# Attention's uses of one PSUM bank set apart, two activations kept on chip, and splits and conversions spread

## The chip, the cores and the metric

One core of a Trainium2 chip. The metric is the device time of one execution in microseconds (us). TensorE is called PE, VectorE DVE, ScalarE ACT, GpSimd POOL and SyncE SP in the rows.

## What is computed

Sliding-window attention for 4 batches of 8 heads (576 positions, 64 per head), then two feed-forward networks over the 2304 tokens:

```python
scores = scale * np.matmul(q, k.transpose(0, 1, 3, 2))
# heads 0-3: 0 <= rel < 32; heads 4-7: 0 <= rel < 128 and rel % 4 == 0
attn = softmax(np.where(masks, scores, -1e9))
x = (attn @ v).transpose(0, 2, 1, 3).reshape(2304, 512)
h = x @ w_in1                                     # 512 -> 2048
x = (np.maximum(h, 0) + alpha * np.minimum(h, 0)) @ w_out1
h = x @ w_in2
g = np.where(h >= 1, h, np.where(h <= -1, 0, (h + 1) ** 2 / 4))
out = g @ w_out2
```

All is float32.

## The kernel before

**Splits.** Every matrix factor is cut into a high and a low part (`two`: ACT copies the high part at L329, DVE or POOL subtracts it at L330), and each product is three matmuls: L514 to L516 for a plain hidden product H, L545 to L547 for a hidden product of the 7-product scheme, L679 to L681 for an output product Y. `xv` is split x, `wr` and `woh`/`wol` are split weights, `gh`/`gl` a split activation.

**Tiles.** The tokens are cut into tiles (network, number): (0,0) 512, (0,1) 256, (0,2) 512, (0,3) 1024, (1,0) 1024, (1,1) 1024, (1,2) 256 tokens. There are 16 feature blocks f per tile.

**Slots.** Tiles (0,0), (0,1), (0,2) run in 16 slots each. A slot f is: H of block f (`f_h`), an attention point, the activation of f (`f_g`: ACT L644, DVE L647, ACT L654; `f_cut` L660 subtracts), Y of block f-2 (`f_y`), another attention point. The 18 attention groups after batch 0 are spread over these points by two tables: `STARTS` says at which point a group's scores begin, `STAGES` how many points later its further steps come. A group is: `s_ps` (scores, PE L147; DVE adds the mask at L151, takes the maximum at L154, subtracts it at L160, ACT takes exp at L161), `t_ps` (PE L214 turns the probabilities, ACT L216 copies them to `pT`), `o_ps` (PE L225 by v; DVE L231 to L233 normalises), `x_ps` (PE L240 turns back; ACT L258 copies to `XA`). All four PE results of every group use one and the same PSUM bank, tag "a".

**Weights.** Network weights arrive on SP's in-order queue (`st`, L274), DVE rewrites the bits of each with three integer operations (`w_cut`, `conv`: L323, L324, L317), and results that are needed later go to DRAM (`whole<-wf`, L301) and come back (`wb<-whole` L351, `wo<-whole` L1075).

**Pairs.** (0,3), (1,0) and (1,1) are computed as two halves of 512 tokens with seven products in place of eight. `x_seven` makes and splits the sums of x (DVE L453 makes a sum in `room`, `two` splits it); `more_x(k)` issues k pieces of that list. Eight steps `p_h` make two feature blocks each for both halves; the first half's Y are issued between, the second half's activations go to DRAM (`gd<-XA`, L624) and are read back (`gx<-gd`, L629) for a "second half" of 16 Y blocks. The first half's last Y and the second half's first ones stand at the border between. In the first pair's second half DVE also converts the last weights of the second network; `HELD` lists the blocks that are not converted there.

**Last.** (1,2) runs in slots again.

Each engine runs its instructions in the order in which the program issues them.

Of the kernel before, what the change touches and what calls it, by code (L numbers as in the profile page):

```python
# [22 lines left out]
P = 128  # L23
# [41 lines left out]
STARTS = (1, 6, 10, 14, 18, 22, 26, 30, 37, 43, 49, 55, 61, 66, 70, 74, 78, 82)  # L65
STAGES = ((3, 4, 6), (2, 3, 5), (3, 5, 8))
# [4 lines left out]
HELD = [f for f in range(NF) if f < 4 or f >= NF - 2]  # L71
# [15 lines left out]
def attention_then_two_ffns(ctx: ExitStack, tc: tile.TileContext, a0, aqk, av, w1i, w1o, w2i, w2o, alpha, masks, ident, out):  # L87
# [68 lines left out]

    def a_exp(i):
        src, s, mx = sc_t.pop(i)
        if i < 4 * NGB:
            nc.vector.tensor_tensor(s, src, mx[:, :, None].to_broadcast([P, 2 * GS, KEYS]), ALU.subtract)  # L160
            nc.scalar.activation(s, s, AF.Exp, scale=SCALE)  # L161
            s_t[i] = s
            return
        nc.vector.tensor_scalar(mx, mx, -SCALE, None, ALU.mult)
        for n in range(2 * GS):
            nc.scalar.activation(s[:, n], src[:, n], AF.Exp, bias=mx[:, n:n + 1], scale=SCALE)
        s_t[i] = s
# [214 lines left out]
    def p_weights(n, p, i):  # L382
# [7 lines left out]
        def other(j):  # L390
            t = wt[n, p, j] = r_slot((n, p, j))
            if n == PAIRS[2]:
                nc.sync.dma_start(t.bitcast(F32), kept[p, j])
                return
            two(t[:, 0], t[:, 1], sums[n, p][:, 2 * j - 2:2 * j].rearrange("p a b -> p (a b)"), on)
            if n == PAIRS[1]:
                kept[p, j] = kept_p.tile([P, 2, DM], F32, tag=f"k{p}_{j}", name="kept")
                nc.sync.dma_start(kept[p, j], t.bitcast(F32))
# [34 lines left out]
    def x_seven(n, room):  # L433
# [13 lines left out]
        def plain(i, k, j, m):  # L447
            return lambda: split(i, m, src(k, j, m), nc.vector if n == PAIRS[0] and i > 3 else nc.gpsimd)
# [80 lines left out]
    def p_h(q, p, after, between):  # L529
# [32 lines left out]
        def top(j, k):  # L562
# [39 lines left out]
        product(c, 2, 1, 5, False)  # L602
        act(1, 0, d)
# [5 lines left out]
        between(2)  # L609
        top(0, 1)  # L610
# [14 lines left out]

    def g_load(n, f):
        tag = x_free.pop(0)
        t = pools[tag].tile([P, 2, TW], F32R, tag=tag, name="gx")
        nc.sync.dma_start(t.bitcast(F32), gd[n, f])  # L629
        gt[(n, 1), f] = (t[:, 0], t[:, 1])  # L630
        g_tags[n, f] = tag
# [30 lines left out]
    def f_y(key, f):  # L662
# [7 lines left out]
        if f == 0:  # L670
# [5 lines left out]
        for c in range(NC):  # L676
            o = yt[key][c][:, :w]
            cs = slice(c * P, (c + 1) * P)
            nc.tensor.matmul(o, wl[:, cs], gh[:, :w], start=(f == 0), stop=False)  # L679
            nc.tensor.matmul(o, wh[:, cs], gh[:, :w], start=False, stop=False)  # L680
            nc.tensor.matmul(o, wh[:, cs], gl[:, :w], start=False, stop=(f == NF - 1))  # L681
        if part:
            x_free.append(g_tags.pop((n, f)))
        if f == NF - 1:
# [18 lines left out]
    with tc.manual_schedule(), ExitStack() as late:  # L703
# [66 lines left out]
        def start(i):  # L770
            a_scores(i, ps_a, "a", i < 2 * NGB)
            a_load_qk(i + 2)
            a_exp(i)
# [113 lines left out]
        def slot(n, f, k):  # L887
# [66 lines left out]
        for n in PLAIN:  # L954
            for f in range(NF):
                slot(n, f, k)
                k += 1
                if n == PLAIN[0] and f == NF - 3:
# [6 lines left out]
                if n == PLAIN[2] and f == READY - 1:  # L965
                    assert nxt == NG and not at
# [4 lines left out]
        def step(q, p):  # L971
            n = PAIRS[q]
            split_pending()
            end = p == NF // 2 - 1

            def after(i):
                if not end:
                    for k in ((0,), (1, 2), (3,))[i]:
                        p_weights(n, p + 1, k)
                if i == 0:  # L980
# [3 lines left out]
                    if end:  # L984
                        for f in range(3):
                            g_load(n, f)
                elif i == 1 and end:
                    one_y()
                    wo_split((n, 0), NF - 2)
                elif i == 2:  # L990
                    if q == 0:
                        more()

            p_h(q, p, after, lambda k: conv(k) if q == 0 else None)

        for q, n in enumerate(PAIRS):
# [16 lines left out]
            flush()  # L1013
            wo_split((n, 0), NF - 1)
            one_y()
            wo_split((n, 1), 0)
            one_y()
            wo_split((n, 1), 1)
            turn = iter(range(1 << 30))

            def room():
                pool, tag = banks(q, 1)[next(turn) % NC]
                return pool.tile([P, TW], F32, tag=tag, name="room")

            if q == 0:
                w0_tile[0] = room
# [3 lines left out]
                more()  # L1030
# [4 lines left out]
            loaded = 3  # L1035
            if nn in PAIRS:
                x_free.extend(r_free[:2])
                del r_free[:2]
            for f in range(NF):
                if loaded < NF:  # L1040
                    g_load(n, loaded)
                    loaded += 1
                if f + 2 < NF:
                    wo_split((n, 1), f + 2)
                if f == NF - 2:
# [3 lines left out]
                    else:  # L1049
                        pend_y += [((n, 1), f), ((n, 1), f + 1)]  # L1050
# [3 lines left out]
                if nn in PAIRS:  # L1054
                    if f in (5, 13):
                        w_base(nn[0], f // 13)
                    if f == NF - 3:
                        r_free.extend(x_free[:2])
                        del x_free[:2]
                    elif f in (8, 9, 10, 11):  # L1060
                        p_weights(nn, 0, f - 8)
                else:
                    if f == 0:
# [109 lines left out]
```

## Time and profile before

| | |
|---|---|
| median of 3 runs | 886.89 us (885.58 to 887.21) |
| the profiled execution | 881.87 us |
| its span | 880.1 us |
| its mean granted clock | 0.994 |
| PE busy | 839.0 us (95%) |
| DVE, ACT, POOL busy | 552.8, 433.6, 487.8 us |

The profiled execution is 5.0 us shorter than the median of the runs. Its span leaves 41.1 us in which PE has no matmul under way. The waits that PE's instructions show say where most of these lie and what ended each.

### The profile page before, as it was taken

To read this page: it belongs to the slowest core of one execution; us is meant where nothing else is said; L and a number is where in the kernel's file an instruction comes from. 1 tells how busy PE (TensorE), PEld (TensorE's weight loads), DVE (VectorE), ACT (ScalarE), POOL (GpSimd) and SP (SyncE) were. 2 spreads that over 40 slices of the span, in tenths; PEclk is the share of its full clock that TensorE was granted. 3 is DMA by queue.
4 is the path that set the end of the run, shared out by engine and by line. 5 is a ranking of instruction groups with operands and counts; after the bars stand their busy time and mean duration, and the time that the engine had idled before them with its cause. 6 is when DMAs were issued, how large, how long until landed. Compare 5 with 4: busy or idle time off the path is not lost.

```text
span 880.1 us, 14306 instructions
## 1 busy us (share of the span) xinstructions
PE 839.0 (95%) x5328; PEld 688.4 (78%) x5330; DVE 552.8 (63%) x911; ACT 433.6 (49%) x809; POOL 487.8 (55%) x417
## 2 busy tenths in 40 slices
PE   6889997998999999999998999999999999999998
PEld 3667776887777778888876788887788888878898
DVE  4788885653776678676558677676417767640143
ACT  3444444555443555555444356554434545453364
POOL 2455554667343656767467677672772242447486
PEclk9999999999999999999999999999999999999999
DMA  7877644553652013543368663625853553549120
GB/s 291 249 223 224 210 137 151 175 182 104 184 174 86 25 42 127 189 145 144 120 251 316 234 228 137 222 96 192 340 186 130 224 186 131 189 163 351 69 90 25
DMA packets 57045, 152.71 MB, mean 174 GB/s; under 512 B 5776, under 2 KB 13584, under 8 KB 56976
## 3 DMA queue, kind: packets, MB, share of 16 engines
q1 hardware_dynamic: 56688, 151.63, 50.6%
q8 instruction: 42, 0.69, 0.3%
q14 instruction: 27, 0.22, 0.1%
q10 hardware_dynamic: 288, 0.16, 0.1%
HBM read 104.59 MB, written 47.19 MB: 172 GB/s over the span
## 4 chain that ended last, share of the span: by engine, by line
PE 83%; DVE 7%; ACT 4%; issue 2%; POOL 1%; DMA 1%; ACTq 0%; DVEq 0%
PE y L679 13%; PE y L681 13%; PE y L680 13%; PE h_ps L545 8%; PE h_ps L547 8%; PE h_ps L546 8%; PE h_ps L514 5%; PE h_ps L516 4%; PE h_ps L515 4%; PE o_ps L225 2%; PE s_ps L147 1%; PE t_ps L214 1%; POOL wol L330 1%; ACT woh L329 1%; DMA st<-w2o 1%
## 5 line engine op out<-in xcount | busy, mean ns | idle before, releaser
L330 POOL TENSOR_TENSOR wol<-wo,woh 128x512 fp32r<-128x512 f32 x159 | 207.3, 1312 | 98.3 <-ACT woh L329 97.6
L679 PE MATMUL y<-gh,wol 128*128 128x512 f32 (+1 forms) x444 | 163.7, 369 | 4.8 <-POOL wol L330 4.8
L681 PE MATMUL y<-gl,woh 128*128 128x512 f32 (+1 forms) x444 | 160.3, 361 | 0.0
L680 PE MATMUL y<-gh,woh 128*128 128x512 f32 (+1 forms) x444 | 160.1, 361 | 0.0
L330 POOL TENSOR_TENSOR wr<-wb,wr 128x512 fp32r<-128x512 f32 x60 | 77.7, 1294 | 129.9 <-ACT wr L329 129.8
L545 PE MATMUL h_ps<-xv,wr 128*128 128x512 f32 x336 | 131.1, 390 | 1.1 <-POOL wr L330 0.9
L329 ACT ACTIVATE woh<-wo 128x512 fp32r<-128x512 f32 x159 | 96.8, 627 | 69.1 <-PE y L681 53.3
L547 PE MATMUL h_ps<-xv,wr 128*128 128x512 f32 x336 | 130.8, 389 | 0.0
L546 PE MATMUL h_ps<-xv,wr 128*128 128x512 f32 x336 | 130.8, 389 | 0.0
L330 POOL TENSOR_TENSOR wr<-wi,wr 128x512 fp32r<-128x512 f32 x50 | 64.7, 1295 | 101.4 <-ACT wr L329 101.3
L679 PEld LDWEIGHTS y<-gh,wol 128*128 128x128 f32 x444 | 83.8, 189 | 21.8 <-POOL wol L330 7.4
L681 PEld LDWEIGHTS y<-gl,woh 128*128 128x128 f32 x444 | 83.7, 188 | 13.3
L514 PE MATMUL h_ps<-xv,wr 128*128 128x512 f32 (+1 forms) x256 | 91.8, 359 | 2.1 <-DVE g L647 1.8
L680 PEld LDWEIGHTS y<-gh,woh 128*128 128x128 f32 x444 | 83.8, 189 | 12.2
L515 PE MATMUL h_ps<-xv,wr 128*128 128x512 f32 (+1 forms) x256 | 87.4, 342 | 0.2 <-DVE xv L330 0.2
L516 PE MATMUL h_ps<-xv,wr 128*128 128x512 f32 (+1 forms) x256 | 87.3, 341 | 0.0
L679 PE MATMUL y<-gx,wol 128*128 128x512 f32 x192 | 75.6, 394 | 4.0 <-DMA gx<-gd 3.2
L559 ACT ACTIVATE g<-g,half 128x512 f32<-128x512 f32 x64 | 44.8, 723 | 69.1 <-DVE g L558 67.8
L680 PE MATMUL y<-gx,woh 128*128 128x512 f32 x192 | 75.3, 392 | 0.0
L545 PEld LDWEIGHTS h_ps<-xv,wr 128*128 128x128 f32 x336 | 63.1, 188 | 15.6 <-POOL wr L330 1.3
L681 PE MATMUL y<-gx,woh 128*128 128x512 f32 x192 | 75.3, 392 | 0.0
L547 PEld LDWEIGHTS h_ps<-xv,wr 128*128 128x128 f32 x336 | 63.1, 188 | 13.2
(123 smaller groups left out, 1505.5 us busy)
## 6 DMA issues: line engine op xcount, KB each, us to landing
gd<-XA SPq DMA_DIRECT2D x48, 512.0 KB, 4.4
gx<-gd SPq DMA_DIRECT2D x48, 512.0 KB, 6.0
wb<-whole SPq DMA_DIRECT2D x30, 512.0 KB, 4.8
st<-w1i SPq DMA_DIRECT2D x16, 512.0 KB, 4.2
st<-w1o SPq DMA_DIRECT2D x16, 512.0 KB, 5.0
st<-w2i SPq DMA_DIRECT2D x16, 512.0 KB, 4.9
st<-w2o SPq DMA_DIRECT2D x16, 512.0 KB, 4.4
kept<-wr SPq DMA_DIRECT2D x16, 512.0 KB, 2.7
```

The costliest lines, as they stand in the source:

```text
L329: nc.scalar.activation(hi, src, AF.Copy)
L330: low_on.tensor_tensor(lo, src, hi.bitcast(F32), ALU.subtract)
L514: nc.tensor.matmul(ps[:, :w], r[:, 1, cs], x[:, 0, xs], start=(c == 0), stop=False)
L515: nc.tensor.matmul(ps[:, :w], r[:, 0, cs], x[:, 1, xs], start=False, stop=False)
L516: nc.tensor.matmul(ps[:, :w], r[:, 0, cs], x[:, 0, xs], start=False, stop=(c == NC - 1))
L545: nc.tensor.matmul(o, w[:, 1, cs], x[:, 0], start=start and m == 0, stop=False, skip_group_check=not start)
L546: nc.tensor.matmul(o, w[:, 0, cs], x[:, 1], start=False, stop=False, skip_group_check=not start)
L547: nc.tensor.matmul(o, w[:, 0, cs], x[:, 0], start=False, stop=m == 1, skip_group_check=not start)
L559: nc.scalar.activation(t, t, AF.Square, bias=half, scale=0.5)
L679: nc.tensor.matmul(o, wl[:, cs], gh[:, :w], start=(f == 0), stop=False)
L680: nc.tensor.matmul(o, wh[:, cs], gh[:, :w], start=False, stop=False)
L681: nc.tensor.matmul(o, wh[:, cs], gl[:, :w], start=False, stop=(f == NF - 1))
```

## The change

1. **Attention points.** `STARTS` and `STAGES` are replaced, so that two uses of bank "a" never follow one another without an H or a Y block between them.
2. **exp.** `a_exp` is cut in two: DVE's subtraction stays with the scores (`a_less`), ACT's exp is issued one attention point later, behind the copy of an `x_ps` that may stand there.
3. **Second halves.** They begin with blocks 14 and 15 (`SECOND`), whose activations stay in buffers of split x (`g_home`); these two are neither stored nor loaded, and their `woh`/`wol` are those of the first half. So `gd` and `gx` go from 48 to 42 transfers each, and six weight splits fall away. The split of the next weights, and the last two Y of the first half, come earlier, in the last step.
4. **Conversions.** `HELD` is 8 blocks in place of 6, so 8 conversions are left for the first pair's second half in place of 10; their loads are issued by a schedule of their own into two more buffers.
5. **Store of kept weights.** `kept<-wr` is issued a step later (`later`).
6. **Splits of x.** The four of (0,1) are spread over the last four slots of (0,0); two staging buffers are freed three slots earlier. `plain` of (0,3) goes to POOL throughout, that of (1,0) to DVE for its last two products. In the last slots of (0,2) the weights come ahead of `more_x`.

```diff
-STARTS = (1, 6, 10, 14, 18, 22, 26, 30, 37, 43, 49, 55, 61, 66, 70, 74, 78, 82)
-STAGES = ((3, 4, 6), (2, 3, 5), (3, 5, 8))
+STARTS = (1, 6, 10, 14, 18, 22, 26, 31, 37, 43, 49, 55, 61, 67, 71, 75, 79, 83)
+STAGES = {1: (3, 4, 6), 26: (3, 4, 6), 31: (3, 5, 7), 37: (3, 5, 7), 43: (3, 5, 7), 49: (3, 5, 7), 55: (3, 5, 7), 61: (2, 3, 7)}
...
-HELD = [f for f in range(NF) if f < 4 or f >= NF - 2]
+HELD = [f for f in range(NF) if f < 2 or f >= NF - 6]
+SECOND = [NF - 2, NF - 1] + list(range(NF - 2))
...
     def a_exp(i):
-        src, s, mx = sc_t.pop(i)
-        if i < 4 * NGB:
-            nc.vector.tensor_tensor(s, src, mx[:, :, None].to_broadcast([P, 2 * GS, KEYS]), ALU.subtract)
-            nc.scalar.activation(s, s, AF.Exp, scale=SCALE)
...
+        nc.scalar.activation(s_t[i], s_t[i], AF.Exp, scale=SCALE)
...
-            return lambda: split(i, m, src(k, j, m), nc.vector if n == PAIRS[0] and i > 3 else nc.gpsimd)
+            return lambda: split(i, m, src(k, j, m), nc.vector if n == PAIRS[1] and i > 3 else nc.gpsimd)
...
+            elif p == NF // 2 - 1:
+                t = g_home(n, f)
+                hi, lo = t[:, 0], t[:, 1]
...
-            if k:
+            if k and p < NF // 2 - 1:
                 later.append(lambda: g_keep(n, f, XA[:, 2 * j:2 * j + 2, t0:t0 + TW]))
...
+        i = SECOND.index(f) if part else f
+        if n in PAIRS and not part and f in SECOND[:2]:
+            wos[(n, 1), f] = (wh, wl)
...
-                stages = STAGES[2 if 2 * NF <= at[i] < 4 * NF - 4 else 0 if i in (NGB, 2 * NGB) else 1]
+                stages = STAGES.get(at[i], (2, 3, 5))
+                if k == 1:
+                    a_exp(i)
...
-            if n == PLAIN[0] and f == NF - 1:
-                for c in range(NC):
-                    x_split(nn, c)
-            if n == PLAIN[1] and f >= NF - NC:
-                x_split(nn, f - NF + NC, True)
+            if n in PLAIN[:2] and f >= NF - NC:
+                x_split(nn, f - NF + NC, n == PLAIN[1])
...
+                if NF - 4 <= f < NF - 1:
+                    p_weights(nn, 0, f - NF + 4)
                 if f in (9, 10):
                     more_x(3)
                 elif f >= READY:
-                    more_x(5 if f < NF - 1 else len(x_work))
-                if f >= NF - 4:
-                    p_weights(nn, 0, f - NF + 4)
+                    more_x((5, 5, 6, len(x_work))[f - READY])
+                if f == NF - 1:
+                    p_weights(nn, 0, 3)
...
                 elif i == 1 and end:
                     one_y()
                     wo_split((n, 0), NF - 2)
+                    wo_split((n, 0), NF - 1)
+                elif i == 3 and end:
+                    one_y()
+                elif i == 4 and end:
+                    wo_split((n, 1), 0)
...
-            flush()
-            wo_split((n, 0), NF - 1)
             one_y()
-            wo_split((n, 1), 0)
             one_y()
-            wo_split((n, 1), 1)
...
                 if q == 0:
+                    for _ in range((2, 1, 1, 0, 0, 1, 1, 1, 1)[i] if i < 9 else 0):
+                        w_load(*pend_l.pop(0))
```

What it moves, word for word from the order of instructions. PE at the end of tile (0,1), where a group's `x_ps` and the next group's `t_ps` stand; before:

```order
L681 MATMUL y_2021<-gl,woh 128x256
L240 MATMUL x_ps<-idt,o 128x128 x3
L214 MATMUL t_ps<-idt,s 128x128 x3
L514 MATMUL h_ps<-xv,wr 128x512
L515 MATMUL h_ps<-xv,wr 128x512
L516 MATMUL h_ps<-xv,wr 128x512
```

and in the changed kernel (its lines are L237 for L240, L211 for L214, L513 to L515 for L514 to L516, L688 to L690 for L679 to L681):

```order
L515 MATMUL h_ps<-xv,wr 128x256
L237 MATMUL x_ps<-idt,o 128x128 x3
L688 MATMUL y_2012<-gh,wol 128x256
L689 MATMUL y_2012<-gh,woh 128x256
L690 MATMUL y_2012<-gl,woh 128x256
...
L690 MATMUL y_2015<-gl,woh 128x256
L211 MATMUL t_ps<-idt,s 128x128 x3
L513 MATMUL h_ps<-xv,wr 128x512
```

`t_ps` followed `x_ps` at once; now the Y block of 12 matmuls stands between them.

ACT in a slot of tile (0,2), where exp stood ahead of the slot's activation; before:

```order
L161 ACTIVATE s<-s 128x384
L644 ACTIVATE g<-h_ps 128x512
L654 ACTIVATE gh<-h_ps 128x512
L329 ACTIVATE wr<-wi 128x512
L258 ACTIVATE XA<-x_ps 128x96x4
L329 ACTIVATE woh<-wo 128x512
L216 ACTIVATE pT<-t_ps 128x384
```

and in the changed kernel (L255 is the copy of `x_ps`, L164 exp, L650 and L660 the activation, L326 a split's copy, L213 the copy of `t_ps`):

```order
L255 ACTIVATE XA<-x_ps 128x96x4
L164 ACTIVATE s<-s 128x384
L650 ACTIVATE g<-h_ps 128x512
L660 ACTIVATE gh<-h_ps 128x512
L326 ACTIVATE wr<-wi 128x512
L213 ACTIVATE pT<-t_ps 128x384
L326 ACTIVATE woh<-wo 128x512
```

Both are one group's pass: exp and the copy of the earlier group's `x_ps` have become neighbours ahead of the activation.

SP at the border of the first pair's halves; before:

```order
L301 DMA whole<-wf 128x1024
L624 DMA gd<-XA 256x1x512 x4
L629 DMA gx<-gd 128x1024 x3
L624 DMA gd<-XA 256x1x512 x2
L274 DMA st<-w2o 128x1024 x2
L629 DMA gx<-gd 128x1024
L1075 DMA wo<-whole 128x512
```

and in the changed kernel (L298 stores `wf`, L637 loads `gx`, L271 loads `st`, L1099 reads `wo` back):

```order
L298 DMA whole<-wf 128x1024
L271 DMA st<-w2o 128x1024
L628 DMA gd<-XA 256x1x512 x4
L637 DMA gx<-gd 128x1024 x2
L298 DMA whole<-wf 128x1024
L271 DMA st<-w2o 128x1024 x2
L1099 DMA wo<-whole 128x512
L637 DMA gx<-gd 128x1024
```

The last store of `wf` has come to stand right ahead of the first read-back of `wo`, and two `gx` are issued ahead of it where three were.

## Rows read from the trace of the kernel before

**Rows 1.** The page: busy time, share of the span and instructions of each engine.
```profile
PE 839.0 (95%) x5328; PEld 688.4 (78%) x5330; DVE 552.8 (63%) x911; ACT 433.6 (49%) x809; POOL 487.8 (55%) x417
```

**Rows 2.** Waits of PE, whole span: waiting line <- releaser: us, times, longest.
```profile
PE t_ps L214 <- ACT XA L258: 8.7, 6, 2.7
PE y L679 <- POOL wol L330: 4.8, 4, 1.6
PE s_ps L147 <- issue: 3.3, 1, 3.3
PE y L679 <- DMA gx<-gd: 3.2, 2, 1.7
PE o_ps L225 <- ACT pT L216: 3.1, 2, 2.5
...
PE s_ps L147 <- ACT XA L258: 1.2, 2, 0.9
...
PE y L679 <- POOL wr L330: 0.8, 1, 0.8
```

**Rows 3.** Timeline of DVE at 134 us: start, duration, what, [idle before].
```profile
134.75 3.22 DVE L330 TENSOR_TENSOR xv<-XA,xv 128x256 fp32r<-128x256 f32 x4 [1.10 <-ACT xv L329]
```

**Rows 4.** Timeline of ACT and PE at 214 us.
```profile
214.03 0.48 ACT L258 ACTIVATE XA<-x_ps 128x384 f32<-128x384 f32 x1
...
214.56 0.55 PE L214 MATMUL t_ps<-idt,s 128*128 128x128 f32 x3 [2.73 <-ACT XA L258]
```

**Rows 5.** Busy time by stretch: us, PE, PEld, DVE, ACT, POOL, PEclk, DMA, GB/s.
```profile
214.80:219.20 4.40, 4.40 (x15) 3.50 (x14) 0.00 (x0) 1.01 (x2) 2.17 (x2) 0.61 0.02 4
```

**Rows 6.** Timeline of ACT at 41 us, in the first interleaved group.
```profile
40.67 0.53 ACT L161 ACTIVATE s<-s 128x384 f32<-128x384 f32 x1 [0.51 <-DVE s L160]
41.26 0.64 ACT L329 ACTIVATE wr<-wi 128x512 fp32r<-128x512 f32 x1
```

**Rows 7.** Timeline of ACT and PE at 113 us, an undisturbed group.
```profile
113.05 0.53 ACT L258 ACTIVATE XA<-x_ps 128x192 f32<-128x192 f32 x2
...
115.24 0.49 PE L214 MATMUL t_ps<-idt,s 128*128 128x128 f32 x3
```

**Rows 8.** Timeline of PE, DVE, ACT and POOL, 282.8 to 287.4 us, in slots of (0,2).
```profile
282.85 0.48 PE L514 MATMUL h_ps<-xv,wr 128*128 128x512 f32 x1
...
284.17 0.69 DVE L660 TENSOR_TENSOR gl<-h_ps,gh 128x512 fp32r<-128x512 f32 x1
...
284.73 1.29 POOL L330 TENSOR_TENSOR wr<-wi,wr 128x512 fp32r<-128x512 f32 x1 [6.60 <-ACT wr L329]
284.77 1.80 DVE L453 TENSOR_TENSOR room<-XA 128x512 f32<-128x512 f32 x1
...
285.46 0.39 PE L516 MATMUL h_ps<-xv,wr 128*128 128x512 f32 x1
...
286.61 0.60 ACT L329 ACTIVATE xv<-room 128x512 fp32r<-128x512 f32 x1 [1.43 <-DVE room L453]
287.10 0.55 ACT L258 ACTIVATE XA<-x_ps 128x192 f32<-128x192 f32 x2
287.24 0.69 DVE L330 TENSOR_TENSOR xv<-room,xv 128x512 fp32r<-128x512 f32 x1 [0.66 <-ACT xv L329]
```

**Rows 9.** Timeline of POOL and PE at 315 us, the last slots of (0,2).
```profile
314.93 1.74 POOL L330 TENSOR_TENSOR wol<-wo,woh 128x512 fp32r<-128x512 f32 x1
...
316.72 0.50 PE L679 MATMUL y<-gh,wol 128*128 128x512 f32 x1
```

**Rows 10.** Waits of SP's queue, 440 to 492 us, the first pair's second half.
```profile
SPq L274 <- DVE wo L317: 17.6, 7, 4.3
```

**Rows 11.** Waits of SP's queue, whole span.
```profile
SPq L351 <- DMA whole<-wf: 4.1, 2, 2.1
```

**Rows 12.** Tile `gx`, 466 to 492 us: its seven transfers.
```profile
DMA to landing us min/median/max: 5.2/6.4/7.5
```

**Rows 13.** Timeline of DVE at 449 us, a sum made in the second half.
```profile
449.32 0.69 DVE L453 TENSOR_TENSOR room<-XA 128x512 f32<-128x512 f32 x1
```

More of the change, by code (lines that the diff above doesn't have):

```diff
@@ L155, in a_scores, with a_less @@
         sc_t[i] = (src, s, mx)
+    def a_less(i):
+        src, s, mx = sc_t.pop(i)
+        nc.vector.tensor_tensor(s, src, mx[:, :, None].to_broadcast([P, 2 * GS, KEYS]), ALU.subtract)
+        s_t[i] = s
     def a_exp(i):
-        src, s, mx = sc_t.pop(i)
-        if i < 4 * NGB:
-            nc.vector.tensor_tensor(s, src, mx[:, :, None].to_broadcast([P, 2 * GS, KEYS]), ALU.subtract)
-            nc.scalar.activation(s, s, AF.Exp, scale=SCALE)
[L162 to L167, printed above, removed]
+        nc.scalar.activation(s_t[i], s_t[i], AF.Exp, scale=SCALE)
     def e_scores(i):
@@ L396, in other, with keep @@
             if n == PAIRS[1]:
-                kept[p, j] = kept_p.tile([P, 2, DM], F32, tag=f"k{p}_{j}", name="kept")
-                nc.sync.dma_start(kept[p, j], t.bitcast(F32))
+                def keep():
+                    kept[p, j] = kept_p.tile([P, 2, DM], F32, tag=f"k{p}_{j}", name="kept")
+                    nc.sync.dma_start(kept[p, j], t.bitcast(F32))
+                later.append(keep)
         if i == 0:
@@ L602, in p_h @@
         product(c, 2, 1, 5, False)
+        after(3)
         act(1, 0, d)
@@ L609, in p_h @@
         between(2)
+        after(4)
         top(0, 1)
@@ L957, in attention_then_two_ffns @@
                 k += 1
[L958 removed]
+                if n == PLAIN[0] and f == NF - 6:
                     spare += [0, 0]
@@ L965, in attention_then_two_ffns @@
                 if n == PLAIN[2] and f == READY - 1:
-                    assert nxt == NG and not at
+                    assert nxt == NG and not s_t and not pT_t
                     assert not pend_w and not todo and not cv, (pend_w, todo)
@@ L974, in step @@
             end = p == NF // 2 - 1
+            if end and n != PAIRS[2]:
+                x_free.extend(r_free[:2])
+                del r_free[:2]
             def after(i):
                 if not end:
-                    for k in ((0,), (1, 2), (3,))[i]:
+                    for k in ((0,), (1, 2), (3,), (), ())[i]:
                         p_weights(n, p + 1, k)
@@ L984, in after @@
                     if end:
-                        for f in range(3):
-                            g_load(n, f)
+                        g_load(n, 0)
                 elif i == 1 and end:
@@ L989, in after @@
                     wo_split((n, 0), NF - 2)
+                    wo_split((n, 0), NF - 1)
[3 more added lines that the diff above has]
+                    wo_split((n, 1), 0)
                 elif i == 2:
+                    if end:
+                        g_load(n, 1)
                     if q == 0:
+                        if end:
+                            conv(3)
                         more()
-            p_h(q, p, after, lambda k: conv(k) if q == 0 else None)
+            p_h(q, p, after, lambda k: conv(k) if q == 0 and not end else None)
         for q, n in enumerate(PAIRS):
@@ L1029, in attention_then_two_ffns @@
                 pend_w += rest
-                more()
+                for _ in range(2):
+                    st_free.append(x_free.pop())
+                hold = True
             if nn in PAIRS:
@@ L1034, in attention_then_two_ffns @@
                 x_work += [(lambda c=c: x_split(nn, c, True)) for c in range(NC)]
[L1035 to L1041, printed above, removed]
+            loaded = 4
+            for i, f in enumerate(SECOND):
+                if i and loaded < NF:
+                    g_load(n, SECOND[loaded])
                     loaded += 1
-                if f + 2 < NF:
-                    wo_split((n, 1), f + 2)
-                if f == NF - 2:
+                if 1 <= i < NF - 2:
+                    wo_split((n, 1), SECOND[i + 2])
+                if i == NF - 2:
                     more_x(len(x_work))
@@ L1075, in attention_then_two_ffns @@
                         nc.sync.dma_start(wo[1, f], whole[1, 1, f // 2][:, f % 2])
-                    if f + 1 not in HELD:
+                    if i < NF - 1 and SECOND[i + 1] not in HELD:
                         conv(3)
-                    if f == NF - 4:
+                    if i == NF - 4:
                         assert not pend_w and not todo and not cv
```

56 lines of the change are left out of this document (31 added, 25 removed).

## The prediction

> **What bounds the kernel now.** The page comes first: PE is busy for 839.0 us of the span, no other engine for more than 553 [rows 1]. So the time is PE's work plus PE's gaps, and an edit off PE pays only where PE waits for it. The gaps are read next, from the waits of PE over the whole span [rows 2]. There the reader is to see four families. One is attention's bank: `t_ps` waits 8.7 us in six places and `s_ps` 1.2 us in two for ACT's copy of the `x_ps` that used the bank just before, and one `s_ps` waits 3.3 us. The second is the splits at the border of the halves: Y waits for `wol` on POOL, 4.8 us in four. The third is the read-back: Y waits for `gx`, 3.2 us in two, and once 0.8 us for POOL's `wr` right behind. The fourth is `o_ps`, 3.1 us in two, for ACT's `pT`.
>
> Then the timeline shows what each was waiting behind. The 3.3 us wait has no releaser named ("issue"), but while it lasts DVE makes four low parts of x in a row, 3.22 us, ahead of the normalisation that frees the bank [rows 3]. The longest `t_ps`, 2.73 us, starts right after ACT's copy of `x_ps` at 214.03, and that copy stood behind the slot's own activation and a split [rows 4]. After this wait PE's granted clock was 0.61, a mean of its two levels, 1.2 and 2.4 GHz, for a stretch of 4.40 us [rows 5]; a block of 12 matmuls takes 2.8 us at the full one (first to last start 2.61 us, and one more step of 0.23) [rows 8]. That is about 1.7 us more than the wait itself.
>
> **The change part by part.**
>
> *Bank uses apart.* Nothing is added on PE; the same matmuls stand in another order. Where `t_ps` or `s_ps` followed `x_ps` at once, a block of 2.8 us (1.4 for 256 columns) now lies between, and on ACT the copy stands ahead of the slot's activation, behind which it ran up to 2.7 us late. So I take off the whole of 8.7 + 1.2 us [rows 2] and the 1.7 us of slow clock. The 3.3 us go too: a Y block stands there now, and the four splits of x are one in a slot. Of `o_ps`, 2.5 us is the first group's, whose order doesn't change, and 0.6 goes. Sum: 8.7 + 1.2 + 3.3 + 0.6 + 1.7 = 15.5 us. The bounds are nothing and these 15.5.
>
> *exp later on ACT.* The instructions are the same, in another place. In an undisturbed group ACT's copy of `x_ps` starts at 113.05 and takes 0.53, and `t_ps` starts at 115.24 [rows 7]. exp, 0.53 long [rows 6], behind that copy would be over near 114.2, some 1.0 us ahead. The slot's activation starts 0.5 us later for it, and its Y is two slots off, so nothing waits. The first group is the exception: exp ran at 40.67 and a split's copy (0.64) right behind it [rows 6]. Now the copy, which waits for its converted weight, stands ahead, and exp ends some 0.5 us later than `t_ps` can bear. I add 0.5 us (bounds nothing and 1.2, the copy and exp together).
>
> *New neighbours.* At the start of tile (0,1) `pT` stands behind two copies of splits, 0.6 each: I add 0.8 us (bounds nothing and 1.3). In slots 9 to 11 of (0,2) scores now start after slot 9's Y. DVE's mask add then stands behind that slot's low part, the sum and its split: from 284.17 to 287.93 these took 3.76 us [rows 8]. With the mask add of some 0.55 the bank is free 4.3 us after the low part starts. On PE the scores (about 0.8) and one H, 2.8, lie between. If the low part starts 0.7 us behind `s_ps`, one conversion, `x_ps` waits 4.3 + 0.7 - 3.6 = 1.4 us. I add this; the bounds are nothing and 2.1, for two conversions. One slot on `pT` stands behind the copy of a sum, where `XA` stood before (286.61, then 287.10, [rows 8]); that mirrors the `t_ps` wait of 1.9 us in this place, with exp ahead too but the copy begun earlier. I add 1.2 (bounds nothing and 1.9).
>
> *Weights ahead of x in the last slots of (0,2), and four splits more on POOL.* Before, `wol` ended at 316.67 and its Y started at 316.72 [rows 9], with no time to spare. Two splits of x are now ahead of it on POOL in that slot, 1.29 each (as the split at 284.73, [rows 8]), of which POOL's idle time takes part. I add 1.0 us (bounds nothing and 2.6).
>
> *The border of the halves.* `wol` for blocks 14 and 15 is made two steps of the program earlier, and there is none to be made for the second half's first two Y, which reuse them. So the 4.8 us go [rows 2], 0.7 of it by the same spread in (0,1). The two `gx` waits of 3.2 us came while SP stood for 17.6 us at `st`, whose buffers come free with DVE's conversions, with `gx` queued behind it [rows 10]. Two more buffers, two conversions less and an issue schedule of its own take them away, and with them the wait for `wr` behind, 0.8. Sum 8.8 us, bounds 4.8 (the reads stay late) and 8.8. The six pairs of transfers saved save nothing by themselves: no wait is for a busy queue. What is moved past others on SP is the last store of `wf`, and a read-back of it follows at once. SP stands there until the store has landed; two such waits took 4.1 us [rows 11]. The third `gx` is queued behind. It needs 2.1 + 6.4 us, 7.5 at the slowest [rows 12], and about 1 us of issues: 9.5 to 10.6. Four Y blocks, 14, 15, 0 and 1, cover it with 11.2 us. So it costs nothing, but has under 2 us to spare.
>
> *The rest.* The kept store issued later, on SP, lies beside a step of p_h and delays no load that PE waits for now: nothing. The branch with six small exps ran for no group.
>
> *Sum.* 15.5 + 8.8 = 24.3 us off; 0.5 + 0.8 + 1.4 + 1.2 + 1.0 = 4.9 us on; net 19.4 us less. The profiled execution, 881.87 us, becomes 862.5. The median of the runs shown is 5.0 us above it, and I carry the difference over: 886.89 - 19.4 = 867.5 us.
>
> **A rule against the change.** A sum of x took 1.80 us on DVE while POOL was at a split that had started at 284.73 [rows 8], and 0.69 with POOL idle [rows 13]. So putting four splits on POOL while DVE makes sums can cost 1.1 us each time they meet, 4.4 us of DVE's time, and 867.5 + 4.4 = 871.9 us if PE waited for all of it. I don't take it into the sum, since the sums in slot 9 and 10 are priced at 1.80 already and the later ones have POOL's chain, not DVE's, as the last. The Trainium skill (SBUF — State Buffer, section "Who interferes with whom") has this as a rule: a DVE instruction with two SBUF inputs contends with a GpSimd instruction that reads SBUF, and the later one is blocked until the other is through. The two rows above agree with it: POOL's split ended at 286.02, and the sum 0.55 us after.
>
> **The rivals.**
>
> *Slower: exp in front of the activation.* The place is every one of the 18 groups. ACT must do the copy and exp before the activation, and `t_ps` comes up to two blocks later. Rows 7 leave about 1.0 us. If exp ended 2.6 us later than I say, each `t_ps` would wait 1.6 us: 886.9 - 24.3 + 18 x 1.6 = 891.4 us. It decides from 24.3 / 18 = 1.35 us per group. For it: ACT was late by up to 2.7 us in six groups [rows 2]. Against it: those were late by the slot's own activation, which is now behind exp, not ahead. 7 in 100, and 4 more for half of it, no change.
>
> *The waits move on.* PE's stalls in the slots come back at other points, as they do in slots 10 and 11: half of the 15.5 us is lost, 19.4 - 7.7 = 11.7 net, 875 us. For it: DVE and ACT have no less to do. Against it: PE has slack of a block wherever the order is changed. 13 in 100. If no new wait comes at all, it is 24.3 us less, 862.6: 13 in 100.
>
> *The read-back doesn't get better.* `gx` stays late or SP's wait for `whole` makes the third late: 4.0 us of the gain stay, 871.5 us. For it: under 2 us to spare. 13 in 100. *DVE and POOL meet*, as above, 871.9: 5 in 100.
>
> **How the numbers follow.** The forecast, 865 to 870, has 45 in 100. The range of 8 in 10 leaves out the slower case and no change, and part of the half gain: 859 to 879. A change of 0.2% (1.8 us) is about what can be told. Faster: 45 + 13 + 13 + 13 + 5 = 89, of which I give 1 to the same; same 5; slower 7.
>
> **What would show it.** Right: no `t_ps` or `s_ps` waits for L255 in the slots; no Y waits for `wol` or `gx` at the borders; PE's waits in the slots shrink to `o_ps` and one `x_ps` for DVE near slots 9 to 11 of (0,2). Wrong: `t_ps` waiting for L164 in many groups; `gx` waits near 450 to 490; clock below 1 in new stretches of the slots.

## The result, and the profile after

The changed kernel took 860.23 us (median of 4 runs, 859.94 to 860.45); the kernel before took 886.24 us beside it (4 runs). The ratio is 0.9707, 95% interval 0.969 to 0.9724: 26.0 us less. The forecast was 19.4 us less and 867.5 us, with a range of 859 to 879, so the time lies inside, near its fast end. It is faster than the 865 to 870 that was held likeliest, and faster than the 862.6 that was reckoned if no new wait came at all. Between the two profiled executions the span fell from 880.1 to 858.2 us, by 21.9.

The page of the changed kernel, busy time and share of the span by engine:

```profile
PE 837.3 (98%) x5328; PEld 688.7 (80%) x5330; DVE 554.5 (65%) x911; ACT 428.8 (50%) x803; POOL 481.9 (56%) x411
```

PE's busy time is what it was [rows 1], to 2 us; what changed is the rest of the span. The other engines do the same work too, but for the six weight splits less on ACT and POOL. So the gain is in waits, and these are the waits of PE in the changed kernel, from 48 us to the end (waiting line <- releaser: us, times, longest):

```profile
PE y L688 <- POOL wol L327: 3.3, 3, 2.3
PE o_ps L222 <- ACT pT L213: 2.3, 2, 1.5
PE h_ps L513 <- POOL wr L327: 1.7, 1, 1.7
PE x_ps L237 <- DVE s L152: 0.6, 1, 0.6
```

Against [rows 2], every `t_ps` and `s_ps` wait is gone (8.7, 3.3 and 1.2 us), and so are both waits for `gx` and the `wr` wait at the second halves. Of the four waits for `wol` of before (4.8 us) three stood at the borders (4.1) and one, of 0.7, in (0,1); all four are gone. Three others have come, two of them (2.7 us together) in the middle of the first pair's second half, and one of 0.6 us in the last slots of (0,2). New are also 1.7 us at the start of (0,1) and 0.6 us of `x_ps`. Of `o_ps`' two waits, one is the first group's, as before, and one is new, in (0,2).

The two that were forecast for (0,2) are there. DVE, POOL and PE at 268 us:

```profile
267.98 0.86 PE L148 MATMUL s_ps<-qk 128*32 128x128 f32 x24
...
268.07 0.69 DVE L666 TENSOR_TENSOR gl<-h_ps,gh 128x512 fp32r<-128x512 f32 x1
268.63 1.29 POOL L327 TENSOR_TENSOR wr<-wi,wr 128x512 fp32r<-128x512 f32 x1 [4.20 <-ACT wr L326]
268.68 1.80 DVE L452 TENSOR_TENSOR room<-XA 128x512 f32<-128x512 f32 x1
...
271.14 0.69 DVE L327 TENSOR_TENSOR xv<-room,xv 128x512 fp32r<-128x512 f32 x1 [0.67 <-ACT xv L326]
271.75 0.55 DVE L152 TENSOR_TENSOR s<-s_ps,mask 128x384 f32<-128x384 f32 x1
...
272.35 0.55 PE L237 MATMUL x_ps<-idt,o 128*128 128x128 f32 x3 [0.55 <-DVE s L152]
```

From the low part's start to the bank's release are 4.23 us, where 4.3 was reckoned from [rows 8]; but the low part starts 0.1 us behind the scores, not 0.7, and the wait is 0.55, not 1.4.

Part of the gain is the clock. In the changed kernel's profile one stretch after 38 us ran below the upper level, the row of busy time by stretch (us, PE, PEld, DVE, ACT, POOL, PEclk, DMA, GB/s):

```profile
39.60:44.00 4.40, 4.40 (x13) 3.40 (x14) 3.47 (x7) 2.55 (x5) 3.77 (x3) 0.61 1.00 273
```

Before had two in its profile, one at 48.7 us (0.53 for 3.4 us) and the one at 214.8 us [rows 5]. The second, some 1.7 us of full speed, has no counterpart.

### The profile page after: what moved, and what is told of

It is laid out like the page before. It is cut to its first block, busy times and chain, and to the rows that moved or that the text cites. A ratio compares the mean times of both kernels' runs of the same rounds, so it can differ in the third digit from the quotient of the medians.

```text
span 858.2 us, 14266 instructions
## 1 busy us (share of the span) xinstructions
PE 837.3 (98%) x5328; PEld 688.7 (80%) x5330; DVE 554.5 (65%) x911; ACT 428.8 (50%) x803; POOL 481.9 (56%) x411
## 4 chain that ended last, share of the span: by engine, by line
PE 88%; DVE 6%; ACT 2%; issue 2%; DMA 1%; POOL 1%; SPq 0%; ACTq 0%; DVEq 0%
PE y L688 14%; PE y L690 14%; PE y L689 14%; PE h_ps L546 9%; PE h_ps L544 9%; PE h_ps L545 9%; PE h_ps L513 5%; PE h_ps L515 4%; PE h_ps L514 4%; PE o_ps L222 2%; PE s_ps L148 1%; DVE room L452 1%; PE t_ps L211 1%; PE x_ps L237 1%; DVE w_ps L321 1%
## 5 line engine op out<-in xcount | busy, mean ns | idle before, releaser
L327 POOL TENSOR_TENSOR wol<-wo,woh 128x512 fp32r<-128x512 f32 x153 | 200.0, 1314 | 86.5 <-ACT woh L326 86.2
L688 PE MATMUL y<-gh,wol 128*128 128x512 f32 (+1 forms) x444 | 164.0, 369 | 0.6 <-POOL wol L327 0.6
L690 PE MATMUL y<-gl,woh 128*128 128x512 f32 (+1 forms) x444 | 160.2, 361 | 0.0
L326 ACT ACTIVATE woh<-wo 128x512 fp32r<-128x512 f32 x153 | 93.6, 626 | 71.8 <-PE y L690 52.2
L688 PEld LDWEIGHTS y<-gh,wol 128*128 128x128 f32 x444 | 83.7, 189 | 16.7 <-POOL wol L327 2.3
L513 PE MATMUL h_ps<-xv,wr 128*128 128x512 f32 (+1 forms) x256 | 90.7, 354 | 3.8 <-DVE g L653 2.0
L690 PEld LDWEIGHTS y<-gl,woh 128*128 128x128 f32 x444 | 83.6, 188 | 13.4
L514 PE MATMUL h_ps<-xv,wr 128*128 128x512 f32 (+1 forms) x256 | 87.0, 340 | 0.2 <-DVE xv L327 0.2
L515 PE MATMUL h_ps<-xv,wr 128*128 128x512 f32 (+1 forms) x256 | 87.0, 340 | 0.0
L688 PE MATMUL y<-gx,wol 128*128 128x512 f32 x192 | 75.5, 393 | 2.7 <-POOL wol L327 2.7
L690 PE MATMUL y<-gx,woh 128*128 128x512 f32 x192 | 75.3, 392 | 0.0
```

The lines of the kernel that those rows point to most:

```text
L326: nc.scalar.activation(hi, src, AF.Copy)
L327: low_on.tensor_tensor(lo, src, hi.bitcast(F32), ALU.subtract)
L513: nc.tensor.matmul(ps[:, :w], r[:, 1, cs], x[:, 0, xs], start=(c == 0), stop=False)
L514: nc.tensor.matmul(ps[:, :w], r[:, 0, cs], x[:, 1, xs], start=False, stop=False)
L515: nc.tensor.matmul(ps[:, :w], r[:, 0, cs], x[:, 0, xs], start=False, stop=(c == NC - 1))
L688: nc.tensor.matmul(o, wl[:, cs], gh[:, :w], start=(i == 0), stop=False)
```

## The experiments

Where a run is called slower or faster than the changed kernel, its median is set against 860.23 us. The changed kernel was not run again beside them, and the median of the kernel before moved from 886.24 to 882.74 us over the comparisons, so a difference of a few us counts only where the waits bear it out.

**The kernel before, once more.** The runs of before lie up to 5 us above its own profiled execution, 881.87. Is that the clock, or does a profiled execution run shorter?

Nothing is edited.

> The kernel before, unchanged, profiled and timed once more. Its profiled execution was 881.87 us, its runs 885.1 to 887.2. Theory one, the slow clock: PE falls to its lower level behind some of its waits, not the same ones each time, at 1.6 to 1.8 us for each fall; then the runs of before lie 3 to 5 us above the first profile because they had two or three falls more, and this profile shows other or more stretches of slow clock than the two (at 49 and 215 us), with a mean clock below 0.994. Theory two: a profiled execution is shorter by itself; then it is near 882 us again with the same two stretches. Ratio to the kernel before 0.998 to 1.002 by both.

The median was 884.99 us (10 runs, 880.51 to 887.47), ratio 1.0004 (0.998 to 1.0028). The profiled execution was 881.57 us, with a mean clock of 0.99. Its waits from 48 us on are those of [rows 2], but for `gx` (4.4 us in three, and no `wr` behind) and the first group's `o_ps`; its stretches of slow clock are others:

```profile
39.70:44.30 4.60, 4.60 (x14) 3.64 (x15) 4.08 (x7) 3.21 (x6) 3.77 (x3) 0.63 1.03 287
...
138.80:142.50 3.70, 3.70 (x13) 2.92 (x10) 2.38 (x4) 1.01 (x2) 0.00 (x0) 0.54 0.61 159
214.80:219.20 4.40, 4.05 (x23) 3.56 (x24) 0.00 (x0) 1.90 (x4) 2.76 (x3) 1.00 0.01 4
```

At 214.8 us the clock is full this time, behind the same 2.7 us wait, and it fell at 139 us, behind the 3.3 us wait, where it had not. So the fall is not bound to a place. The two profiled executions took nearly the same time (881.87 and 881.57 us) at mean clocks of 0.994 and 0.990. Over the 23 runs of this comparison a lower mean clock goes with a longer time, but loosely: 880.27 us at 0.994, 884.81 at 0.988 and 887.30 at 0.983, yet 880.51 and 886.51 both at 0.990. So theory one, more slow stretches in the longer runs, can be a part of it at most, and it is not shown: no long run of this kernel was profiled. Theory two has the other kernels against it: in conv_later, plain_back and best_a the profiled execution was the longest of the four runs. Why both profiled executions of before lie among its short ones stays open.

**The attention points undone.**

```diff
-STARTS = (1, 6, 10, 14, 18, 22, 26, 31, 37, 43, 49, 55, 61, 67, 71, 75, 79, 83)
+STARTS = (1, 6, 10, 14, 18, 22, 26, 30, 37, 43, 49, 55, 61, 66, 70, 74, 78, 82)
+STAGES = ((3, 4, 6), (2, 3, 5), (3, 5, 8))
...
             a_less(i)
+            a_exp(i)
...
-                if k == 1:
-                    a_exp(i)
...
```

> The changed kernel with its attention points undone: the old two tables and exp right behind the subtraction; all else as changed. If the bank's neighbours made the waits, most of 8.7 + 1.2 + 0.6 us come back, with one or two stretches of slow clock, and the 0.6 and 0.8 us that are new in the (0,2) slots go: 869 to 874 us. The 3.3 us wait comes back in part at most, as the splits of x stay spread. Rival, the other edits (splits, conversions) made the room on ACT and DVE: under 864 us, with fewer than three t_ps waits.

873.19 us (872.78 to 875.03), ratio to before 0.988 (0.9854 to 0.9907): 13.0 us more than the changed kernel's 860.23. Waits of PE, 108 to 300 us:

```profile
PE t_ps L211 <- ACT XA L255: 8.7, 6, 2.7
PE s_ps L148 <- issue: 2.0, 1, 2.0
PE o_ps L222 <- ACT pT L213: 1.3, 2, 0.6
PE s_ps L148 <- ACT XA L255: 1.1, 2, 0.9
```

The same six `t_ps` waits are back, to the tenth. The neighbours in the bank made most of them: exp_at_start below, with the new tables and exp in its old place, has one `t_ps` wait, 1.5 us. One thing to see beside: the `s_ps` wait is 2.0 us, not 3.3, though the splits of x are spread here. Spreading alone would have left most of it.

**The attention points alone**, on the kernel before.

```diff
-STARTS = (1, 6, 10, 14, 18, 22, 26, 30, 37, 43, 49, 55, 61, 66, 70, 74, 78, 82)
+STARTS = (1, 6, 10, 14, 18, 22, 26, 31, 37, 43, 49, 55, 61, 67, 71, 75, 79, 83)
...
-            a_exp(i)
+            a_less(i)
...
+                if k == 1:
+                    a_exp(i)
...
```

(`STAGES` and the two halves of `a_exp` are as in the change.)

> The kernel before with the attention points and the later exp alone. If the order of the bank's uses is what counts, 8.7 + 1.2 + 0.6 + 3.3 us of waits go and one or two of the scattered falls of the clock (1.7 us each), against about 1.5 us of new waits in the (0,2) slots: 868 to 873 us, with no wait at 139 us though four splits of x still stand there. Rival, it needs the other edits' room on DVE and ACT: above 875 us.

868.66 us (867.54 to 870.05), ratio 0.9835 (0.9809 to 0.9861); before had a median of 882.74 beside it, so 14.1 us less. DVE still makes four splits in a row before it normalises, and PE doesn't wait for the bank (timeline of DVE and PE):

```profile
134.30 3.26 DVE L326 TENSOR_TENSOR xv<-XA,xv 128x256 fp32r<-128x256 f32 x4 [1.09 <-ACT xv L325]
...
134.99 0.87 PE L221 MATMUL o_ps<-vz,pT 128*32 128x130 f32 x24
135.79 0.50 PE L675 MATMUL y<-gh,wol 128*128 128x512 f32 x1
...
137.89 0.56 DVE L229 TENSOR_TENSOR o<-o_ps,rs 128x384 f32<-128x384 f32 x1
...
138.75 0.52 PE L147 MATMUL s_ps<-qk 128*32 128x128 f32 x10
```

DVE frees the bank at 138.45. In the kernel before it did so at 138.87, behind the splits of [rows 3]; now a Y block lies in front of the scores, and they start at 138.75 with no wait. The 0.7 us wait for `wol` in (0,1) is gone here too, and back in old_points: it went with the points.

**exp right behind the subtraction**, the new tables kept.

```diff
             a_less(i)
+            a_exp(i)
...
-                if k == 1:
-                    a_exp(i)
```

> The changed kernel with exp right behind the subtraction, at the group's first attention point, the new tables kept. If the later place keeps ACT from standing at exp for the subtraction, the slot's activation and the copies come later again: 861 to 865 us, with waits for XA or pT. Rival, the later place makes t_ps late: then it is 1 us or more faster than the changed kernel's 860.2, above all in the first group. If neither matters, 860.2 within 0.8.

863.98 us (862.87 to 864.62), ratio 0.9771 (0.975 to 0.9792): 3.75 us more than the changed kernel. Waits of PE from 48 us:

```profile
PE o_ps L222 <- ACT pT L213: 3.3, 3, 1.7
PE y L688 <- POOL wol L327: 3.0, 2, 2.4
PE t_ps L211 <- ACT XA L255: 1.5, 1, 1.5
PE x_ps L237 <- DVE s L152: 1.2, 2, 0.6
PE h_ps L513 <- POOL wr L327: 0.8, 1, 0.8
```

`t_ps`, `x_ps` and `o_ps` wait about 3 us more in sum. The `t_ps` wait can be followed back to exp, with two splits and the copy of `x_ps` queued behind it (timeline of ACT and PE):

```profile
203.22 0.53 ACT L164 ACTIVATE s<-s 128x384 f32<-128x384 f32 x1 [2.13 <-DVE s L160]
...
204.69 0.47 ACT L255 ACTIVATE XA<-x_ps 128x384 f32<-128x384 f32 x1
...
205.21 0.55 PE L211 MATMUL t_ps<-idt,s 128*128 128x128 f32 x3 [1.50 <-ACT XA L255]
```

The longest `o_ps` wait, 1.7 us, has the copy of a sum ahead of `pT`, as the 0.8 of the changed kernel has; that exp lengthens it is not shown. The group of the 18 exps in this kernel, then in the changed one (busy, mean ns | idle time before them and what ended most of it):

```profile
L164 ACT ACTIVATE s<-s 128x384 f32<-128x384 f32 x18 | 9.5, 526 | 29.7 <-DVE s L160 29.7
```

```profile
L164 ACT ACTIVATE s<-s 128x384 f32<-128x384 f32 x18 | 9.5, 526 | 0.4 <-DVE s L160 0.3
```

In the early place ACT stands 29.7 us for the subtraction, in the late one 0.4. Most of that standing only moves: from 48 to 300 us ACT waits 22.1 us for PE's `x_ps` in the changed kernel and 4.7 here. What counts is what is queued behind. This speaks against the rival with exp late on ACT: the later place costs less than the early one.

**The splits of x in the last slot again.**

```diff
-            if n in PLAIN[:2] and f >= NF - NC:
-                x_split(nn, f - NF + NC, n == PLAIN[1])
+            if n == PLAIN[0] and f == NF - 1:
+                for c in range(NC):
+                    x_split(nn, c)
...
```

(The split for (0,2) stays; the two buffers are freed at `NF - 3` again.)

> The changed kernel with the four splits of x for (0,1) back in the last slot of (0,0), and the two staging buffers freed three slots later, as before; the new attention points kept. If a Y block between two uses of the bank is enough cover, the 3.22 us that the four splits take on DVE are hidden but for some 0.5 us: 860 to 861.5 us. Rival, the spreading itself took the 3.3 us wait away: 862.5 to 864 us with a wait at the bank near 139 us.

859.91 us (859.81 to 859.95), ratio 0.9733 (0.9713 to 0.9753): no difference to the changed kernel, and no wait at the bank. The spreading earns nothing once the points are changed. There was no wait for `wr` at 150 us in it either.

**The old order of the second halves.**

```diff
-SECOND = [NF - 2, NF - 1] + list(range(NF - 2))
+SECOND = list(range(NF))
...
-            elif p == NF // 2 - 1:
-                t = g_home(n, f)
-                hi, lo = t[:, 0], t[:, 1]
...
+            wo_split((n, 1), 1)
             turn = iter(range(1 << 30))
...
```

(The reads of `gx` and the loads of the conversions, not shown, stand sooner as the order needs.)

> The changed kernel with its second halves in the old order: blocks 14 and 15 are stored and loaded like the others, their weights are split again, and the splits for the second half's first Y stand at the border. The last two Y of the first half stay early, and the conversions keep their own schedule, two slots sooner as the order needs. If the splits at the border made the wol waits, 1.0 to 1.6 us come back at each of three borders: 863 to 866 us. Rival, it was the earlier place of the last two Y: then 860 to 861.5 and no wait at the second and third border.

870.03 us (869.2 to 873.19), ratio 0.9847 (0.9821 to 0.9874): 9.8 us more, over what either expected. PE's waits of 480 us to the end:

```profile
PE y L683 <- POOL wol L327: 2.1, 2, 1.1
```

The second and third border have their `wol` waits back, 1.1 and 1.0 us; the rival said none. At the first border and in the middle of the half that follows it Y waits 8.8 us for `wol` in two, 5.5 the longer. There this kernel differs in two things, the border's splits and the conversions two slots sooner, and it doesn't tell them apart.

**The loads of the conversions as before.**

```diff
-                for _ in range(2):
-                    st_free.append(x_free.pop())
-                hold = True
+                more()
...
-                    for _ in range((2, 1, 1, 0, 0, 1, 1, 1, 1)[i] if i < 9 else 0):
-                        w_load(*pend_l.pop(0))
...
```

> The changed kernel with the loads of the first pair's second half issued as before, each when a conversion frees a buffer, and without the two buffers more; the 8 conversions and the new order of the halves kept. If gx was late because SP stood at these loads, Y waits for gx again, 3 to 4.5 us, and the two waits for wol (2.3 and 0.4 us) may go: 861 to 865 us. Rival, two conversions less and two activations at home are enough: 859 to 861 us and no wait for gx.

860.57 us (858.51 to 862.25), ratio 0.9739 (0.9714 to 0.9765): the same time. PE's waits, 440 to 490 us, in this kernel, and in the same stretch of the changed one:

```profile
PE y L688 <- DMA gx<-gd: 2.4, 2, 1.8
```

```profile
PE y L688 <- POOL wol L327: 2.7, 2, 2.3
```

So the theory had the cause right (SP stands 19.2 us at these loads here, with `gx` behind it) and the balance wrong: the schedule takes 2.4 us of `gx` away and gives 2.7 us of `wol` back.

**The next pair's weights first.** Where the 2.3 us come from is in the changed kernel's ACT and POOL:

```profile
457.66 1.09 ACT L326 ACTIVATE xv<-room 128x512 fp32r<-128x512 f32 x2 [2.69 <-DVE room L452]
458.63 0.64 ACT L326 ACTIVATE wr<-wb 128x512 fp32r<-128x512 f32 x1
...
459.35 1.30 POOL L327 TENSOR_TENSOR wr<-wb,wr 128x512 fp32r<-128x512 f32 x1 [3.01 <-ACT wr L326]
460.60 0.74 POOL L403 TENSOR_TENSOR ss<-wb 128x256 f32<-128x256 f32 x1
...
463.49 1.26 POOL L327 TENSOR_TENSOR wol<-wo,woh 128x512 fp32r<-128x512 f32 x1
...
464.81 0.50 PE L688 MATMUL y<-gx,wol 128*128 128x512 f32 x1 [2.30 <-POOL wol L327]
```

POOL stands 3.0 us for `wr`, whose copy stands on ACT behind a sum that DVE has not made, and the `wol` that Y needs is queued behind `wr` and four sums. The edit issues `wr` ahead of the pieces of x:

```diff
                 f_y((n, 1), f)
+                if nn in PAIRS and i in (8, 9, 10, 11):
+                    p_weights(nn, 0, i - 8)
                 more_x(2)
...
-                    elif i in (8, 9, 10, 11):
-                        p_weights(nn, 0, i - 8)
```

> The changed kernel with the next pair's weights issued ahead of the two pieces of x_seven in slots 8 to 11 of each second half that has them. If the 2.3 us wait for wol came from POOL standing at wr, whose copy stood on ACT behind the split of a sum that DVE had not made, the waits of 2.3 and 0.4 us go: 857 to 858.5 us. Rival, POOL simply has too much in these slots: the wait moves to another Y, 859.5 to 861 us.

858.37 us (858.29 to 859.05), ratio 0.9717 (0.9697 to 0.9738): 1.9 us less than the changed kernel. The waits between 440 and 490 us are 1.4 us (0.9 and 0.5) in place of 2.7, not gone. What is left of the first has the same cause one copy on; POOL stands again, for `woh`, whose copy stands on ACT behind a sum:

```profile
463.37 0.60 ACT L326 ACTIVATE xv<-room 128x512 fp32r<-128x512 f32 x1 [3.48 <-DVE room L452]
463.86 0.62 ACT L326 ACTIVATE woh<-wo 128x512 fp32r<-128x512 f32 x1
...
464.56 1.27 POOL L327 TENSOR_TENSOR wol<-wo,woh 128x512 fp32r<-128x512 f32 x1 [1.43 <-ACT woh L326]
...
465.89 0.50 PE L688 MATMUL y<-gx,wol 128*128 128x512 f32 x1 [0.92 <-POOL wol L327]
```

**A conversion step out of the first slot of (0,1).** The wait of 1.7 us at 150 us begins on DVE, which stands 4.93 us for a load:

```profile
146.57 0.69 DVE L320 TENSOR_SCALAR w_ps<-st 128x512 int32<-128x512 int32 x1 [4.93 <-DMA st<-w2i]
147.18 0.48 DVE L653 SCALAR_TENSOR_TENSOR h_ps<-g,al,h_ps 128x256 f32<-128x256 f32 x1
...
147.69 0.38 ACT L660 ACTIVATE gh<-h_ps 128x256 fp32r<-128x256 f32 x1 [2.43 <-DVE h_ps L653]
147.97 1.14 ACT L326 ACTIVATE wr<-wi 128x512 fp32r<-128x512 f32 x2
...
149.99 0.39 PE L513 MATMUL h_ps<-xv,wr 128*128 128x256 f32 x1 [1.70 <-POOL wr L327]
```

```diff
-                ops = 1 if n == PLAIN[1] else 3
+                ops = (0 if f == 0 else 2 if f == 1 else 1) if n == PLAIN[1] else 3
```

> The changed kernel with the first slot of (0,1) left without a conversion step and the second slot given two. If the 1.7 us wait for wr at 150 us came from DVE standing at a conversion for a load that had not landed, with the slot's activation and then the copy for wr behind it, it goes: 858 to 859 us. Rival, the wait moves one slot on with the conversion: 859.8 to 861 us.

859.72 us (859.07 to 860.23), ratio 0.9728 (0.9703 to 0.9753). No wait for `wr` at 150 us is left; the gain, 0.5 us of the median, is less than the wait and lies between what the two expectations said. x_old_spread has no such wait either, without this edit.

**The unsummed splits back on their old engines.**

```diff
-            ... nc.vector if n == PAIRS[1] and i > 3 else nc.gpsimd)
+            ... nc.vector if n == PAIRS[0] and i > 3 else nc.gpsimd)
```

> The changed kernel with the last unsummed splits of x on their old engines: those of the first pair on DVE, those of the second on POOL. If POOL is what comes last in the first pair's second half, four more splits there make the two waits for wol longer: 861 to 864 us. Rival, splits on POOL block DVE's sums in the last slots of (0,2): then the 0.6 us wait for wol at 303 us goes, and the time is 858.5 to 859.8 us.

861.77 us (860.5 to 864.02), ratio 0.9755 (0.9733 to 0.9778): 1.5 us more. That is the time of the first expectation, but not its mechanism. The `wol` waits in the second half are 2.6 us, as before the edit (2.7). The 0.6 us at 303 us did go, and a wait of 1.8 us for DVE's `gl` came at 312 us, in the step behind; that is about the whole difference.

**What adds up.** `best_a` is weights_first with x_old_spread; best_b is that with conv_later:

```diff
+                    p_weights(nn, 0, i - 8)
                 more_x(2)
...
+            if n == PLAIN[0] and f == NF - 1:
+                for c in range(NC):
+                    x_split(nn, c)
...
+                ops = (0 if f == 0 else 2 if f == 1 else 1) if n == PLAIN[1] else 3
```

> The changed kernel with the weights first (as in weights_first) and the splits of x for (0,1) in the last slot again (as in x_old_spread), which had no wait for wr at 150 us. If the two add up, that wait's remaining 0.5 us goes and those at 465 and 469 us stay at 0.9 and 0.5: 857.3 to 858.3 us. Rival, the fall of the clock takes the place of what is gained: 858.3 to 859.3.

> best_a with the conversion step moved out of the first slot of (0,1) too. The wait that it aims at is gone already in best_a, so the same time within 0.5 us if no other conversion comes late for it; if one does (at 352 us there was such a wait of 0.2), up to 0.5 us more.

best_a took 858.12 us (857.32 to 860.02), ratio 0.9722 (0.9701 to 0.9743); best_b 856.73 us (855.87 to 857.89), ratio 0.9704 (0.9685 to 0.9723). best_b is 3.5 us faster than the changed kernel by the medians of different comparisons. By their ratios to the kernel before the two are alike (0.9704 and 0.9707), as before itself took 882.74 us beside the one and 886.24 beside the other; what speaks for a gain is the waits below, 4.9 us where the changed kernel has 7.9. I had expected nothing from the third edit; but in best_a the `wr` wait was there, 0.8 us. It comes and goes with the landing of the load: DVE stood 4.93 us for it in the changed kernel, 4.67 in best_a and 3.96 in x_old_spread, which had no wait. So x_old_spread had not removed its cause. In best_b, PE's waits from 48 us on are

```profile
PE o_ps L222 <- ACT pT L213: 2.3, 2, 1.4
PE y L688 <- POOL wol L327: 2.0, 3, 0.9
PE x_ps L237 <- DVE s L152: 0.6, 1, 0.6
```

## Why the prediction was right, and where it was off

The time, the sign and the main mechanism held, the bank's uses set apart and the waits at the borders and for `gx` taken off. One step had the wrong sign, one missed a wait, and the terms at their measured sizes come to less than was gained, so the time lies where it does in part by what no term holds. By its own steps:

- **Bank uses apart, 15.5 us.** Right in its waits. Those named are gone and come back when the points are undone; with the later exp the points alone gave 14.1 us (with the new waits in (0,2) in it), and undoing both cost 13.0. The two can be told apart: old_points and exp_at_start both have exp in the early place and differ in the tables alone, 873.19 and 863.98 us in the same comparison. So the tables are worth 9.2 us there, and the 3.75 us between exp_at_start and the changed kernel are exp's.
- **exp later, +0.5 us in the first group, else nothing.** The sign was wrong: with exp at its old place the kernel is 3.75 us slower. The rows of an undisturbed group [rows 7] showed the room for a later exp; that the early one holds ACT while DVE makes the subtractions (45.5 us in the kernel before) I did not price. In the first group `t_ps` does wait for exp where the clock doesn't slow PE just ahead, 0.2 to 0.3 us (x_old_spread, weights_first, conv_later).
- **New neighbours, 0.8 + 1.4 + 1.2 us.** In (0,2) 0.55 and 0.85 us, at the places and with the releasers named. At the start of (0,1) not `pT` but `wr` waited, 1.7 us, and for a late load, which I had not followed. That is over the bound of 1.3 us for this place.
- **Weights ahead of x, 1.0 us.** 0.6 us, for `wol`, in the place named.
- **The border, 8.8 us.** The waits for `wol` (4.1 us at the borders) and for `gx` went, and undoing the new order brought 1.1 and 1.0 us back at two borders. The 0.7 us in (0,1), which the prediction puts down to the spread, went with the attention points. The read-back behind the last store cost PE nothing. But 2.7 us came for `wol` in the middle of the half. I looked at SP there and not at ACT and POOL, where the copies stand behind sums that DVE has not made.
- **The rule on DVE and POOL.** Not what decided: with the splits back on their old engines the time rose by 1.5 us rather than fell. A sum that meets a split on POOL is seen in the 1.80 us again: POOL's split starts at 268.63, and the sum ends 0.56 us after it (the 0.69 of [rows 13] was not with POOL idle throughout, as I wrote: a split began at 449.74, 0.42 us after the sum); but the 12 sums of this kind were no slower for the change, with a median of 1.19 us before, 1.12 in the changed kernel and 1.21 in plain_back.
- **The clock, 1.7 us, and the 5.0 us carried over.** In the profiles the first held, with one slow stretch less. Waits taken off: 8.7 + 1.2 + 3.3 + 0.6 + 4.8 + 3.2 + 0.8 = 22.6 us; waits put on: 1.7 + 0.6 + 0.8 + 3.3 = 6.4, where 4.9 were forecast. The net, 16.2, with one stretch of 1.7 us is 17.9, less than the 19.4 forecast. Three things that I had not forecast make up the profiled spans' 21.9: the first group's `o_ps` waits 1.5 us where it waited 2.5, the waits ahead of it fell from 11.0 to 9.1 in sum, and three short waits of H, 1.3 in sum, are gone (17.9 + 1.0 + 1.9 + 1.3 = 22.1). The first two are not the change's: in before_again, the same kernel as before, that group waits 1.0 us and the waits ahead of it come to 8.8. They differ as much between two executions of one kernel. Against before_again the spans differ by 21.6 all the same, for there PE is busy for 841.7 us, 2.7 more than in the first profile, with as many slow stretches after 38 us; what that is stays open. The medians differ by 26.0, another 4 us, because I carried the 5.0 us between profile and median over to the new kernel, where it is 0.3. Why it does not carry is not shown. It is not that kernels without the bank's waits scatter less: four runs of the changed kernel lie within 0.5 us and four of x_old_spread within 0.2, but those of best_b spread over 2.0, plain_back 3.5 and old_loads 3.7. Nor is it the mean clock alone: plain_back's longest run had 0.994, its shortest 0.992. How much of the 26.0 is there for good depends on the runs of before that stand beside it: its median was 884.81, 883.52 and 882.74 us in the three later comparisons, so 22.5 to 24.6 us against those.

Open is what the first border alone would cost without activations at home, what the later store of kept weights does, since no run has it alone, and what makes some runs of before longer than others.

## What to carry to other kernels

Where one bank passes through several engines, look at what stands between two uses of it on the engine that waits: a block of other work there took away waits that spreading the other engines' work left. An instruction that is queued early and waits for another engine holds all that is queued behind it; its price is read from that, not from its own place. When a wait goes, follow the in-order queues of every engine that the edit touches, one step on, not only the one that was late. And a sum of waits from one profile against one other holds what two executions of the same kernel differ by; a second profile of the kernel before shows how much that is.

## What was not expected of the hardware

After a wait of 2.7 us the granted clock was 0.61 for 4.4 us in one execution and full in another of the same program, and after one of 3.3 us 0.54 for 3.7 us in the second and full in the first. It is the same behind the 2.3 us wait for `wol` in the first pair's second half: 1.00 for the 4.0 us from 464.8 us in the changed kernel, 0.57 for the 4.0 us from 465 us in x_old_spread, where the wait ends at 463.85. x_old_spread's four runs lie within 0.2 us nevertheless.
